# A second Strassen level for the last product of a down projection, with helper work moved to GpSimd

## The chip, the cores and the metric

The kernel runs on one core of one Trainium2 chip. The metric is the device time of one execution in microseconds, lower is better. I use two measures side by side: the ratio of timed runs (with a 95% interval), and the lengths of the program's stages on TensorE's timeline.

The engines are called PE (TensorE matmul), PEld (its weight loads), DVE (VectorE), ACT (ScalarE), POOL (GpSimd) and SP (the queue that issues the DMAs) in profile lines. SBUF is the on-chip memory that holds the operands; PSUM is the memory that TensorE writes its results to, in banks. In the lines of the down stage, `ps` stands for PSUM, `RE` for the partial results `U` and `V`, `RO` for sums on their way to an output, `RX` for residual and output tiles, `RAB` for operand sums and for the outputs of product 5.

## The reference, cut to what matters

```python
def reference(A_x, A_wqkv, A_wo, B_x, B_W_gate, B_W_up, B_W_down):
    ...
    x = A_x                                            # [1, 2048, 1024] bf16
    h = x + _A_ref(_layernorm(x), A_wqkv, A_wo)        # linear attention, 32 heads
    h2 = h + _B_ref(_layernorm(h), B_W_gate, B_W_up, B_W_down)
    return h2
# _B_ref: gate, up = x @ W_gate, x @ W_up  (1024 x 3584); (relu(gate) * up) @ W_down  (3584 x 1024)
```

Only the last product, with `W_down`, and the addition of `h` are touched by the change.

## The kernel before

The token axis is handled in two passes of 1024 tokens. Each pass has a gate/up stage of 14 pairs of feature tiles (PE 12.09 us per pair), then a down stage. Every large product uses Strassen's scheme: seven half-size block products in place of eight. In the down stage the seven products run one after the other. Four are "direct" (56 matmuls with 512 columns); three are split a second time by the same scheme into seven half products of 14 matmuls with 256 columns ("level 2"). The program numbers the products 0 to 6.

Operands of level 2 are sums of blocks. Activation sums are made by VectorE during the down stage. Weight sums are made once, in gate/up pass 0, and stored to DRAM.

```python
            direct(0, XB, a_hh(0, 0), False, True, e_s1)
            level2(1, q_d2, sg_ro, ev(0, B_U, 0, B_U, "dU"))
            direct(2, XB, a_hh(1, 0), False, False, e_11)
            level2(3, q_hh(0, hh16), sg_x0, ev(STB, B_V, 0, B_U, "dV"))
            direct(4, XB, a_d1(), True, True, e_22)
            level2(5, q_hh(1, hh), sg_x0, ev_21)
            direct(6, XB, a_hh(1, 0, hh16), False, False, e_12)      # the product that the change splits
```

`U` and `V` are f32 partial results in SBUF. After product 4, VectorE adds the result banks to `V` (`e_22`), and GpSimd adds four residual tiles of `h` to make four outputs. The residuals for the two other output blocks are added into `V` and `U` by VectorE:

```python
            def e_22(j):
                h, hb = hv(1, 1, j)
                tt(dsum[:, j, :], bank(XB[j]), V_[j], [B_bank[XB[j]], B_V[j]], [B_dsum[j]], "d22")
                put(1, 1, j, dsum[:, j, :], h, [B_dsum[j], hb], "pool")
            ...
            def add_h(dst, bufs_, blk, dh):
                for j in range(STB):
                    h, hb = hv(blk, dh, j)
                    tt(dst[j], dst[j], h, [hb], [bufs_[j]], "dh")      # VectorE, two SBUF inputs
            ...
            at(4, 0, lambda: ld_h(1, 1))          # "after unit (product, part): load residual tiles"
            at(4, 2, lambda: ld_h(1, 0))
            ...
            at(5, 0, lambda: add_h(V_, B_V, 1, 0))
            at(5, 6, lambda: ld_h(0, 1))
            at(6, 2, lambda: add_h(U_, B_U, 0, 1))
```

Inside a level-2 product four PSUM banks are reused: a later half product goes on accumulating in a bank that VectorE reads, so PE may not start it before that read is over.

```python
                def m5():
                    prod(5, c, sg(0), False)
                    evac(5, c)
                ...
                def m3():
                    prod(3, c, sg(3), False)
                    evac(3, c)
                units.extend(((pi, i), f_) for i, f_ in enumerate((m1, m7, m6, m2, m5, m4, m3)))
```

The whole DMA work goes through one in-order queue (SP). Down-stage weights come through a ring of 7 slots in pass 0 and 13 in pass 1.

## Time and profile before

| | before |
|---|---|
| time, median of 3 | 737.76 us (737.58 to 738.92) |
| PE busy | 726.8 us, 99% of 737.5 |
| DVE, ACT, POOL busy | 544.3 us (74%), 350.4 us (48%), 61.3 us (8%) |
| one direct product, PE | 12.09 us |
| one level-2 product, PE | 10.70 us |

The page's first part gives the busy times and, after the `x`, the instructions:

```profile
PE 726.8 (99%) x4227; PEld 356.0 (48%) x4227; DVE 544.3 (74%) x972; ACT 350.4 (48%) x610; POOL 61.3 (8%) x125
```

A busy PE is not by itself a PE at its limit, but the timeline says more. In PE's timeline of down pass 0 (start, length in us, engine, line, operation, tiles, count, and in brackets idle time before it with its releaser) the end of the stage looks like this:

```profile
465.34 1.69 PE L687 MATMUL ps<-RAB 128*128 128x256 f16 x14
466.87 3.22 PE L687 MATMUL ps<-RE,RAB 128*128 128x256 f16 x28
469.93 9.46 PE L687 MATMUL ps<-RW,RAB 128*128 128x256 f16 x50
479.23 2.75 PE L687 MATMUL ps<-RAB 128*128 128x512 bf16 x12
481.82 1.89 PE L687 MATMUL ps<-RE,RAB 128*128 128x512 bf16 x8
484.08 1.90 PE L687 MATMUL ps<-RH,RWG 128*128 128x512 bf16 x8 [0.37 <-DVE RX L1399]
```

A half product starts 1.53 us after the one before it (465.34 to 466.87), and the only idle time is 0.37 us at the border to gate/up pass 1, where the first bank waits for the last output add. (A named idle time counts from the modelled end of the matmul before. Counted from start to start, the border costs 0.54 us; the waits of the down stage below are likewise about 0.16 us longer from start to start than named.) So each microsecond of matmul taken away should come off the time, unless another engine then arrives too late.

VectorE's and GpSimd's timelines show what those engines do around products 4 to 6 of pass 0 (VectorE first):

```profile
449.48 4.34 DVE L1399 TENSOR_TENSOR RAB<-RAB 128x1792 f16<-128x1792 bf16 x4
459.66 2.48 DVE L1399 TENSOR_TENSOR RO<-ps,RE 128x512 f32<-128x512 f32 x4 [5.85 <-PE ps L687]
462.24 4.79 DVE L1399 TENSOR_TENSOR RE<-RE,RX 128x512 f32<-128x512 f32 x4
...
479.79 2.50 DVE L1399 TENSOR_TENSOR RE<-RE,RX 128x512 f32<-128x512 f32 x4 [3.92 <-DMA RX<-h_scr]
```

```profile
460.49 5.39 POOL L1399 TENSOR_TENSOR RX<-RO,RX 128x512 bf16<-128x512 f32 x4 [93.63 <-DVE RO L1399]
```

The two `RE<-RE,RX` lines are the same four VectorE adds with two SBUF inputs. Beside GpSimd's adds (460.49 to 465.88) they take 4.79 us, without them 2.50 us. This is the trace's form of what the Trainium skill says in "SBUF — State Buffer", section "Who interferes with whom": a VectorE instruction with two SBUF inputs and a GpSimd instruction that reads SBUF exclude each other.

### The profile page before, as it was taken

How to read it: one execution, taken by the hardware profiler on the slowest of the kernel's cores; microseconds unless marked ns; L12 is line 12 of the kernel's file. 1: busy time of each engine (PE TensorE's matmuls, PEld its weight loads, DVE VectorE, ACT ScalarE, POOL GpSimd, SP SyncE). 2: the span in 40 equal slices, each digit the busy share in tenths (PEclk: the TensorE clock that was granted, in tenths of full speed). 3: DMA queues.
4: the chain of work that ended last, by engine and by line, in shares of the span. 5: the costliest groups of instructions: out<-in, count | busy, mean ns of one | idle time of the engine just before them, and what ended most of it. 6: DMA issues, size and time to landing. Idle time of an engine off the chain costs nothing.

```text
span 737.5 us, 11324 instructions
## 1 busy us (share of the span) xinstructions
PE 726.8 (99%) x4227; PEld 356.0 (48%) x4227; DVE 544.3 (74%) x972; ACT 350.4 (48%) x610; POOL 61.3 (8%) x125
## 2 busy tenths in 40 slices
PE   7999999999999999999999999999999999999998
PEld 3444444344444444444444666744444444447764
DVE  6886877799776988888987765775757575676563
ACT  3877756864841457777754100035454454521000
POOL 1311100000360001110100000200000000000020
PEclk9999999999999999999999999999999999999999
DMA  9635135113999887797869999952424242337872
GB/s 309 204 72 101 28 96 167 39 26 64 192 234 256 269 249 226 234 282 229 261 203 286 315 251 324 328 173 73 110 63 114 58 116 57 100 109 246 239 223 85
DMA packets 185302, 129.32 MB, mean 175 GB/s; under 512 B 51488, under 2 KB 168224, under 8 KB 185248
## 3 DMA queue, kind: packets, MB, share of 16 engines
q1 hardware_dynamic: 184576, 127.95, 61.5%
q8 instruction: 33, 0.54, 0.3%
q10 hardware_dynamic: 672, 0.66, 0.3%
q14 instruction: 21, 0.17, 0.1%
HBM read 93.72 MB, written 23.33 MB: 159 GB/s over the span
## 4 chain that ended last, share of the span: by engine, by line
PE 90%; DVE 5%; ACT 2%; DMA 2%; issue 1%; DVEq 0%; SPq 0%; ACTq 0%
PE ps L687 90%; DVE RAB L773 1%; ACT RX L766 1%; DVE RE L1148 1%; DMA RE<-in_A_x_dram 1%; DMA RAB<-RXH 1%; DVE RX L770 1%; DVE RX L989 0%; ACT ps L692 0%; ACT RXH L725 0%; PE ps L830 0%; DVE rden L1146 0%; DVE st L701 0%; DVE RX L1399 0%; DVE RWG L908 0%
## 5 line engine op out<-in xcount | busy, mean ns | idle before, releaser
L692 ACT ACTIVATE ps<-ps 128x512 f32<-128x512 f32 x168 | 97.8, 582 | 205.5 <-PE ps L687 145.6
L687 PE MATMUL ps<-RC,RO 128*128 128x512 f16 x672 | 154.2, 379 | 0.0
L687 PE MATMUL ps<-RH,RWG 128*128 128x512 bf16 x448 | 105.8, 379 | 0.4 <-DVE RX L1399 0.4
L687 PEld LDWEIGHTS ps<-RC,RO 128*128 128x128 f16 x672 | 65.8, 98 | 79.3
L1322 DVE TENSOR_TENSOR RAB<-ps,RAB 128x512 bf16<-128x512 f32 x56 | 38.6, 689 | 77.3 <-PE ps L687 77.3
L687 PE MATMUL ps<-RC,RWG 128*128 128x512 f16 x320 | 76.8, 379 | 0.1
L1318 DVE TENSOR_TENSOR RE<-ps,RE 128x512 bf16<-128x512 f32 x112 | 74.3, 684 | 1.7 <-PE ps L687 0.7
L687 PEld LDWEIGHTS ps<-RH,RWG 128*128 128x128 bf16 x448 | 43.8, 98 | 53.5 <-DVE RX L1399 0.9
L687 PE MATMUL ps<-RW,RAB 128*128 128x512 bf16 (+2 forms) x378 | 67.6, 336 | 0.0
L692 ACT ACTIVATE RE<-RE 128x512 bf16<-128x512 bf16 x56 | 35.1, 627 | 61.1 <-DVE RE L1318 60.5
L687 PE MATMUL ps<-RH,RO 128*128 128x512 bf16 (+1 forms) x256 | 61.2, 379 | 0.0
L687 PE MATMUL ps<-RW,RE 128*128 128x512 bf16 x256 | 57.5, 379 | 0.8 <-DVE RXH L1172 0.7
L687 PE MATMUL ps<-RAB 128*128 128x512 bf16 (+1 forms) x252 | 54.8, 357 | 0.0
L692 ACT ACTIVATE RE<-ps 128x512 f32<-128x512 f32 x64 | 37.7, 597 | 35.7 <-PE ps L687 35.3
L687 PEld LDWEIGHTS ps<-RW,RAB 128*128 128x128 bf16 (+1 forms) x378 | 37.0, 98 | 28.8
L687 PEld LDWEIGHTS ps<-RC,RWG 128*128 128x128 bf16 (+1 forms) x320 | 30.0, 98 | 39.9 <-ACT ps L692 5.9
L692 ACT ACTIVATE RAB<-ps 128x512 bf16<-128x512 f32 x56 | 33.4, 596 | 15.7 <-PE ps L687 14.6
L1266 DVE TENSOR_TENSOR RO<-RWG 128x1024 f16<-128x1024 bf16 x54 | 36.9, 683 | 4.7 <-DMA RWG<-in_B_W_up_dram 4.7
L1399 POOL TENSOR_TENSOR RX<-RO,RX 128x512 bf16<-128x512 f32 x8 | 10.8, 1379 | 338.4 <-DVE RO L1399 338.4
L687 PEld LDWEIGHTS ps<-RH,RO 128*128 128x128 f16 (+1 forms) x256 | 24.4, 98 | 30.1 <-ACT RX L692 1.6
L687 PEld LDWEIGHTS ps<-RW,RE 128*128 128x128 bf16 x256 | 23.9, 98 | 28.9 <-DVE RXH L1172 1.2
L1266 DVE TENSOR_TENSOR RO<-RWG,RO 128x1024 f16<-128x1024 bf16 x54 | 37.0, 686 | 1.0
(138 smaller groups left out, 944.0 us busy)
## 6 DMA issues: line engine op xcount, KB each, us to landing
RWG<-in_B_W_gate_dram SPq DMA_DIRECT2D x28, 512.0 KB, 4.8
RWG<-in_B_W_up_dram SPq DMA_DIRECT2D x28, 512.0 KB, 5.8
RW<-in_B_W_down_dram SPq DMA_DIRECT2D x14, 512.0 KB, 5.1
t_scr<-RW SPq DMA_DIRECT2D x14, 512.0 KB, 5.0
RE<-in_A_x_dram SPq DMA_DIRECT2D x23, 256.0 KB, 3.7
l_scr<-RX SPq DMA_DIRECT2D x7, 768.0 KB, 4.5
RW<-in_B_W_down_dram SPq DMA_DIRECT2D x14, 384.0 KB, 5.9
h_scr<-RXH SPq DMA_DIRECT2D x16, 256.0 KB, 3.3
```

The lines of the kernel that those rows point to most:

```text
L687: lambda e: e.matmul(out_ap, lhsT, rhs, start=start, stop=stop, skip_group_check=skip),
L692: PL.add("act", lambda e: e.activation(out=dst, in_=src, func=func), reads=reads, writes=writes, name=name)
L766: PL.add("act", lambda e: e.activation(out=Et[:, k, :], in_=src, func=ACTF.Exp), reads=[src_buf], writes=[B_E[k]], name=name + "_exp")
L770: PL.add("dve", lambda e: e.tensor_scalar(out=Et[:, k, :], in0=Et[:, k, :], scalar1=1.0, scalar2=1e-6, op0=ALU.min, op1=ALU.add), reads=[] ...
L773: PL.add("dve", lambda e: e.scalar_tensor_tensor(out=dst_ap, in0=src, scalar=C1, in1=Et[:, k, :], op0=ALU.add, op1=ALU.max), reads=[src_bu ...
L1148: PL.add("dve", lambda e: e.tensor_tensor(out=osb[:, k, :].rearrange("p (g h e) -> p g h e", h=HPG, e=Dh), in0=nv[:, :, :, 0:Dh], in1=rden ...
L1266: PL.add(eng, lambda e: e.tensor_tensor(out=tb(j, u), in0=f0(u), in1=f1(u), op=ALU.subtract), reads=[B_w[i + x] for x in r] + ([B_T[k + x] ...
L1318: PL.add("dve", lambda e: e.tensor_tensor(out=dst, in0=src, in1=ftmp[:, w, :], op=ALU.add), reads=[bsrc, B_s5[w]], writes=[bdst], name=name)
L1322: PL.add("dve", lambda e: e.tensor_tensor(out=dst, in0=a_, in1=b_, op=ALU.mult), reads=reads, writes=[wr], name=name)
L1399: PL.add(eng, lambda e: e.tensor_tensor(out=dst, in0=in0, in1=in1, op=op), reads=reads, writes=writes, name=name)
```

## The change

The intent: product 6 also gets a second level (56 x 512 columns become 7 x 14 x 256). Its weight sums are extra work in gate/up pass 0; they go to GpSimd because VectorE is busy there. The residual adds into `U` and `V` go to GpSimd, earlier than before, so that the outputs of products 5 and 6 can be written straight from PSUM.

```diff
-        WSRC = [("b", 0, 0), ("l", 1), ("b", 1, 0), ("l", 2), ("t", 0), ("l", 3), ("b", 1, 1)]
+        WSRC = [("b", 0, 0), ("l", 1), ("b", 1, 0), ("l", 2), ("t", 0), ("l", 3), ("l", 4)]
...                                      # in wd_sums (VectorE weight sums of one raw pair)
-            if q + NWR < NPAIR:
-                load_wraw(q + NWR)
...
+            def addw(j, x, y):
+                PL.add("pool", lambda e: e.tensor_tensor(out=lsw[:, z, j, :], in0=x[0], in1=y[0], op=ALU.subtract),
+                       reads=x[1] + y[1], writes=[B_lsw[z][j]], name="WM%d_%d" % (j, m))
+            def raw():
+                addw(0, wr(0, 1), wr(0, 0))
+                addw(2, wr(1, 1), wr(0, 1))
+                addw(1, wr(1, 1), t_(0))
+                addw(3, wr(1, 0), t_(1))
+                dma(sl_lw[z], l_v[:, no, :, m, :], lsw[:, z], "st_wm_%d" % m, reads=B_lsw[z], writes=[B_wscr[m]])
...
-                    tt(dst[j], dst[j], h, [hb], [bufs_[j]], "dh")
+                tt(dst[j], dst[j], h, [hb], [bufs_[j]], "dh", eng="pool")
...
-            direct(6, XB, a_hh(1, 0, hh16), False, False, e_12)
+            level2(6, XB, q_d4, sg_x1, ev_out(0, 1, 0, B_U, outst, B_outst, sl_out))
...
-            at(4, 0, lambda: ld_h(1, 1))
+            at(3, 4, lambda: ld_h(0, 1))
+            at(4, 0, lambda: ld_h(1, 1), *[lambda j=j: add_h(U_, B_U, 0, 1, j) for j in range(STB)])
             at(4, 2, lambda: ld_h(1, 0))
-            for i in range(4):
-                at(4, i, sg4[i])
-            at(5, 0, lambda: add_h(V_, B_V, 1, 0))
-            at(5, 6, lambda: ld_h(0, 1))
-            at(6, 2, lambda: add_h(U_, B_U, 0, 1))
+            for i, f_ in enumerate(sg4 + sg3):
+                at(4, i // 2, f_)
+            order = (2, 3, 0, 1)
+            at(5, 0, *[lambda j=j: add_h(V_, B_V, 1, 0, j) for j in order], *[lambda j=j: p_22(j) for j in range(STB)],
+               lambda: e_u5(0), lambda: e_u5(1))
+            at(5, 1, lambda: e_u5(2), lambda: e_u5(3))
+            at(5, 4, st_flush)
```

VectorE now has eight operand sums during product 4 (`sg4 + sg3`) where it had four. The raw rows of `W_down` are loaded two at a time, after GpSimd has read the pair before.

More of the change, by code (lines that the diff above doesn't have):

```diff
@@ L199, in bass_sequential_preLN__linear_attn_block__glu_gated_reglu__prompt_kernel @@
     t_v = t_scr.rearrange("(o p) (q c) -> p o q c", p=P, c=NW)
-    l_scr = nc.dram_tensor("l_scr", [len(L2O) * 4 * P, WDW], f16).ap()
+    l_scr = nc.dram_tensor("l_scr", [(len(L2O) + 1) * 4 * P, WDW], f16).ap()
     l_v = l_scr.rearrange("(o j p) (m c) -> p o j m c", p=P, j=4, c=HNW)
@@ L238, in bass_sequential_preLN__linear_attn_block__glu_gated_reglu__prompt_kernel @@
         hh = RAB[:, 0:NFT * TOK].rearrange("p (a b) -> p a b", a=NFT)
-        wdx = RAB[:, NFT * TOK + 4 * SBW:NFT * TOK + 4 * SBW + WDW]
+        wdx = RAB[:, NFT * TOK + 4 * SBW:NFT * TOK + 8 * SBW]
+        lsw = wdx.bitcast(f16).rearrange("p (s j c) -> p s j c", s=2, j=4)
         o0 = NFT * TOK
@@ L253, in bass_sequential_preLN__linear_attn_block__glu_gated_reglu__prompt_kernel @@
         wo = RW[:].rearrange("p (a b) -> p a b", a=NG)
-        wdring = [RW[:, i * WDW:(i + 1) * WDW] for i in range(NWS - 3)] + [wdx]
+        wdring = [RW[:, i * WDW:(i + 1) * WDW] for i in range(NWS - 3)] + [wdx[:, 0:WDW]]
         D2 = RC[:, 0:NPAIR * SBW].bitcast(f16).rearrange("p (q t) -> p q t", t=SBW)
@@ L372, in bass_sequential_preLN__linear_attn_block__glu_gated_reglu__prompt_kernel @@
         sl_ls = slots("dls_", 2)
+        sl_lw = slots("dlw_", 2)
         sl_out = slots("dout_", NOS)
@@ L433, in bass_sequential_preLN__linear_attn_block__glu_gated_reglu__prompt_kernel @@
         B_lscr = bufs("lscr_", NM)
+        B_lsw = [bufs("lsw%d_" % i, 4) for i in range(2)]
+        B_wscr = bufs("wscr_", NM)
         B_sgo = bufs("sgo_", 4)
@@ L472, in bass_sequential_preLN__linear_attn_block__glu_gated_reglu__prompt_kernel @@
             b_.over = B_wraw + flat(B_wsum)
-        B_wd[NWS - 3].over = flat(B_xnT) + flat(B_pqT)
+        for b_ in flat(B_lsw):
+            b_.over = flat(B_xnT) + flat(B_pqT)
+        B_wd[NWS - 3].over = flat(B_lsw)
         for b_ in B_wd[NWS - 2:NWS]:
@@ L614, in load_wd_next @@
             if src[0] == "l":
-                dst = dst.rearrange("p (m c) -> p m c", c=HNW)
+                dst = dst[:, 0:WDW].rearrange("p (m c) -> p m c", c=HNW)
                 o = src[1]
-                if src[2] == "q":
+                if src[2] == "q" and o == 4:
+                    k, h = src[3:]
+                    dma(sl_wd[i], wdring[i].rearrange("p (m c) -> p m c", c=HNW),
+                        wd_v[:, 1, k:NPAIR:2, NW + h * HNW:NW + (h + 1) * HNW], "ld_wr_%d" % L, writes=[B_wd[i]])
+                elif src[2] == "q":
                     k, h = src[3:]
@@ L621, in load_wd_next @@
                 else:
-                    dma(sl_wd[i], dst, l_v[:, L2O.index(o), src[3]], "ld_wl_%d" % L, reads=B_lscr,
+                    dma(sl_wd[i], dst, l_v[:, o - 1, src[3]], "ld_wl_%d" % L, reads=B_wscr if o == 4 else B_lscr,
                         writes=[B_wd[i]])
@@ L679, in half, with wr, t_ @@
                     add(3, wq_(1, 0), t(1))
-                    dma(sl_ls[z], l_v[:, :, :, m, :], lsum[:, z], "st_wl_%d" % m, reads=B_lsum[z],
+                    dma(sl_ls[z], l_v[:, 0:no, :, m, :], lsum[:, z], "st_wl_%d" % m, reads=B_lsum[z],
                         writes=[B_lscr[m]])
-            return [lambda: half(0), lambda: half(1)]
+            def wr(k, h):
+                return wraw[:, (2 * m + k) % NWR, 1, NW + h * HNW:NW + (h + 1) * HNW], [B_wraw[(2 * m + k) % NWR]]
+            def addw(j, x, y):
+                PL.add("pool", lambda e: e.tensor_tensor(out=lsw[:, z, j, :], in0=x[0], in1=y[0], op=ALU.subtract),
+                       reads=x[1] + y[1], writes=[B_lsw[z][j]], name="WM%d_%d" % (j, m))
+            def raw():
+                def t_(j):
+                    return lsw[:, z, j, :], [B_lsw[z][j]]
+                addw(0, wr(0, 1), wr(0, 0))
[3 more added lines that the diff above has]
+                dma(sl_lw[z], l_v[:, no, :, m, :], lsw[:, z], "st_wm_%d" % m, reads=B_lsw[z], writes=[B_wscr[m]])
+            return [lambda: half(0), lambda: half(1), raw]
         def mm(out_ap, lhsT, rhs, start, stop, reads, bbuf, name, skip=False):
@@ L1383, in bass_sequential_preLN__linear_attn_block__glu_gated_reglu__prompt_kernel @@
         X0v = hh16[:, 0:NFT:2, 0:SBW]
+        X1v = hh16[:, 0:NFT:2, SBW:2 * SBW]
         def down_pass(ps_, fill):
@@ L1431, in e_22, with p_22, e_u5, add_h @@
             def e_22(j):
+                tt(dsum[:, j, :], bank(XB[j]), V_[j], [B_bank[XB[j]], B_V[j]], [B_dsum[j]], "d22")
+            def p_22(j):
                 h, hb = hv(1, 1, j)
-                tt(dsum[:, j, :], bank(XB[j]), V_[j], [B_bank[XB[j]], B_V[j]], [B_dsum[j]], "d22")
                 put(1, 1, j, dsum[:, j, :], h, [B_dsum[j], hb], "pool")
-            def e_12(j):
-                put(0, 1, j, bank(XB[j]), U_[j], [B_bank[XB[j]], B_U[j]])
-            def add_h(dst, bufs_, blk, dh):
-                for j in range(STB):
-                    h, hb = hv(blk, dh, j)
-                    tt(dst[j], dst[j], h, [hb], [bufs_[j]], "dh")
+            def e_u5(j):
+                tt(U_[j], bank(XB[j]), U_[j], [B_bank[XB[j]]], [B_U[j]], "dU5")
+            def add_h(dst, bufs_, blk, dh, j):
+                h, hb = hv(blk, dh, j)
+                tt(dst[j], dst[j], h, [hb], [bufs_[j]], "dh", eng="pool")
             def quad(base, T, H):
@@ L1452, in l2_add, with l2_out @@
                    bd[2 * T:2 * T + 2], name)
-            def l2_out(T, H, b):
-                tt(out2[:, 2 * T:2 * T + 2, H * HNW:(H + 1) * HNW], qb(b), quad(STB, T, H),
-                   [B_bank[b]] + B_V[2 * T:2 * T + 2], B_out2[2 * T:2 * T + 2], "out21_%d%d" % (T, H))
+            def l2_out(ost, bo, base, bs, T, H, b):
+                tt(ost[:, 2 * T:2 * T + 2, H * HNW:(H + 1) * HNW], qb(b), quad(base, T, H),
+                   [B_bank[b]] + bs[2 * T:2 * T + 2], bo[2 * T:2 * T + 2], "out_%d%d" % (T, H))
             def a_hh(k, t, f=hh):
@@ L1499, in sg_x0, with sg_x1, q_d4 @@
                 return X0v[:, b0:b0 + NM, c0:c0 + SHB], [B_hh[2 * (b0 + m)][0] for m in range(NM)]
+            def sg_x1(j):
+                b0, c0 = NM * (j // 2), (j % 2) * SHB
+                return X1v[:, b0:b0 + NM, c0:c0 + SHB], [B_hh[2 * (b0 + m)][1] for m in range(NM)]
+            def q_d4(k, t):
+                i0 = 2 * k + 1
+                return hh16[:, i0:NFT:4, t * SHB:(t + 1) * SHB], [B_hh[i][0] for i in range(i0, NFT, 4)]
             units = []
@@ L1523, in go @@
                                 evac(j)
-                                if pi == 6:
-                                    st_flush()
                         else:
@@ L1531, in direct, with level2 @@
                     units.append(((pi, ci), go))
-            def level2(pi, Q, sg, evac):
-                a, f, b, c = YB
+            def level2(pi, bks, Q, sg, evac):
+                a, f, b, c = bks
                 def prod(mi, bk, x, start):
@@ L1539, in prod @@
                     wd_use[0] += 1
-                    w = wdring[ws].bitcast(f16)
+                    w = wdring[ws]
+                    if pi != 6 or mi in (5, 6, 7, 4):
+                        w = w.bitcast(f16)
                     for m in range(NM):
@@ L1594, in ev, with ev_out, out, st @@
                 return go
-            def ev_21(m, b):
-                if m == 2:
-                    l2_out(0, 0, b)
-                elif m == 7:
-                    l2_add(STB, B_V, STB, B_V, 1, 1, b, "dV2")
-                    l2_add(STB, B_V, STB, B_V, 1, 0, b, "dV2")
-                elif m == 5:
-                    l2_out(1, 1, b)
-                elif m == 4:
-                    l2_out(1, 0, b)
-                    for j in (2, 3):
-                        st_out(1, 0, j, sl_out2[j], out2[:, j, :], B_out2[j])
-                elif m == 3:
-                    l2_out(0, 1, b)
-                    for j in (0, 1):
-                        st_out(1, 0, j, sl_out2[j], out2[:, j, :], B_out2[j])
+            def ev_out(blk, dh, base, bs, ost, bo, sl):
+                def out(T, H, b):
+                    l2_out(ost, bo, base, bs, T, H, b)
+                def st(T):
+                    for j in (2 * T, 2 * T + 1):
+                        st_out(blk, dh, j, sl[j], ost[:, j, :], bo[j])
+                def go(m, b):
+                    if m == 2:
+                        out(0, 0, b)
+                    elif m == 7:
+                        l2_add(base, bs, base, bs, 1, 1, b, "dA")
+                        l2_add(base, bs, base, bs, 1, 0, b, "dA")
+                    elif m == 5:
+                        out(1, 1, b)
+                    elif m == 4:
+                        out(1, 0, b)
+                        st(1)
+                    elif m == 3:
+                        out(0, 1, b)
+                        st(0)
+                return go
             direct(0, XB, a_hh(0, 0), False, True, e_s1)
-            level2(1, q_d2, sg_ro, ev(0, B_U, 0, B_U, "dU"))
+            level2(1, YB, q_d2, sg_ro, ev(0, B_U, 0, B_U, "dU"))
             direct(2, XB, a_hh(1, 0), False, False, e_11)
-            level2(3, q_hh(0, hh16), sg_x0, ev(STB, B_V, 0, B_U, "dV"))
+            level2(3, YB, q_hh(0, hh16), sg_x0, ev(STB, B_V, 0, B_U, "dV"))
             direct(4, XB, a_d1(), True, True, e_22)
-            level2(5, q_hh(1, hh), sg_x0, ev_21)
-            direct(6, XB, a_hh(1, 0, hh16), False, False, e_12)
+            level2(5, YB, q_hh(1, hh), sg_x0, ev_out(1, 0, STB, B_V, out2, B_out2, sl_out2))
+            level2(6, XB, q_d4, sg_x1, ev_out(0, 1, 0, B_U, outst, B_outst, sl_out))
             post = {}
@@ L1638, in down_pass @@
             at(0, 3, sg6[3])
+            sg3 = l2_sums(q_d4, sg_x1, "sg3")
             at(2, 0, lambda: ld_h(0, 0))
-            for key in ((3, 1), (5, 1), (5, 6), (6, 0)):
+            for key in ((3, 1), (5, 6), (6, 0), (6, 6)):
                 at(*key, st_flush)
@@ L1878, in bass_sequential_preLN__linear_attn_block__glu_gated_reglu__prompt_kernel @@
                         if x % 2 == 1:
-                            w0_, w1_ = wl_sums(x // 2)
+                            w0_, w1_, wr_ = wl_sums(x // 2)
                             mid[1].append(w0_)
                             wl_q.append(w1_)
+                            mid[0].append(wr_)
+                            for z in (x + 1, x + 2):
+                                if z < NPAIR:
+                                    mid[0].append(lambda z=z: load_wraw(z))
                     if q not in wt_at:
```

## The prediction

The recorded texts count the products from one: their fifth product is product 4, their sixth is product 5.

> **What bounds the kernel.** TensorE. The page gives PE 726.8 of 737.5 us busy (99%) at a granted clock of 0.998, the chain of waits is 90% PE, and the list of waits holds only about 6.8 us of named PE waits, nearly all before 181 us. From there on PE idles once: 0.37 us at 483.7 us, between down pass 0 and gate/up pass 1, on VectorE's last output add. VectorE (74%), ScalarE (48%) and GpSimd (8%) have room. DMA is not free everywhere: in the stretches of down pass 0 (403 to 484 us) its busy share is 0.93 to 1.14 at about 255 to 325 GB/s; in gate/up pass 0 it is 0.86; at the end of pass 1 only 0.27.
>
> **What the change removes.** The last of the seven Strassen products, 56 matmuls of 512 columns per pass, becomes seven half-size products, 98 matmuls of 256 columns. The PE timeline shows both kinds: a direct product advances at 0.2159 us per matmul, 12.09 us in all; a second-level half product takes 1.528 us (starts 415.19, 416.72, 418.25), so seven take 10.70 us. Weight loads double to 98 but already hide in the existing second-level products (PE idle 0.0). Saving: 1.39 us per pass, 2.8 us in two, all on the critical path. I also expect the 0.37 us gap to go: bank 0 is now emptied four half products before the end. At the very end VectorE now has one add (0.69 us) after the last matmul where it had a queue of four ending 1.3 us after it: 0.2 to 0.5 us.
>
> **What it adds.** (1) GpSimd: 28 weight sums of 256 columns in gate/up pass 0, about 0.6 us each (estimate from the trace's 1.157 us for 512 columns), 17 us; and eight more 1.35 us residual adds per down pass. The Trainium skill ("SBUF — State Buffer", Who interferes with whom) says that a VectorE instruction with two SBUF inputs and a GpSimd instruction that reads SBUF shut each other out. The trace agrees: four such VectorE adds took 4.79 us beside GpSimd at 462 us and 2.50 us alone at 480 us. A gate/up pair has 1.2 to 2.4 us of VectorE idle, against at most 2.4 us of GpSimd sums every second pair: I expect 0 to 0.5 us of PE idle there. (2) DMA: 1.8 MB of stores in gate/up pass 0 (hidden), and weights of the last product 3.2 MB instead of 1.8 MB. (3) In down pass 0 the weight ring is seven ahead and the queue issues in order. The four stores of the GpSimd outputs now stand before the last two weight loads; VectorE has eight 1.09 us sums instead of four in the fifth product, blocked in part by four GpSimd adds, and GpSimd then runs eight adds in series (about 11 us). So the stores go 13 to 16 us after the fifth product's end, the next load lands 4 to 6 us later, and is due at 18.3 us: 0 to 3 us of PE wait, about 1 us expected. Pass 1 has thirteen slots: no wait.
>
> **Sum.** 2.8 + 0.4 + 0.3 − 1.0 − 0.3 = 2.2 us: 735.5 us. Range 734.0 to 737.0. Chances: faster by over 2% 0.01, within 2% 0.97, slower 0.02.
>
> **What would show it.** Last product about 10.7 us of PE in both passes; no gap at the pass boundary; VectorE sums of the fifth product stretched beside GpSimd; a PE wait on a weight load, if any, in the last two half products of pass 0 only; gate/up stretches equal within 0.5 us.
>
> **What would make it wrong.** VectorE, held by GpSimd, delaying gate/up (slower); the late loads waiting longer than 3 us; or neither costing anything (734.2).

## The result, and the profile after

The changed kernel took 736.48 us (median of 4 runs, 735.53 to 737.34), the kernel before 737.67 us (4 runs, 736.38 to 738.92). The ratio is 0.9984 with a 95% interval of 0.9962 to 1.0005: 1.2 us less, not clear of noise. Ratios in this document are the mean time of one kernel's fast runs over that of the other's fast runs of the same rounds, so they are not quite the ratio of the medians.

```profile
PE 720.8 (98%) x4253; PEld 363.2 (49%) x4311; DVE 561.6 (76%) x976; ACT 352.0 (48%) x614; POOL 103.7 (14%) x169
```

(PE has 84 matmuls more in the program, 4311; the trace lacks 58 of their records.) The list of PE's waits (line and tile, releaser; us in total, times, longest) now has entries from the middle of the program, where before there was one of 0.4 us:

```profile
PE ps L710 <- DVE RE L1341: 1.6, 2, 1.1
PE ps L710 <- DVE RAB L1423: 1.0, 1, 1.0
PE ps L710 <- DMA RW<-in_B_W_down_dram: 0.4, 1, 0.4
```

Lines have moved: L710 is the matmul helper (L687 before), L1423 the down stage's elementwise helper (L1399), L1341 the gate/up result adds (L1318), L677 and L655 the VectorE weight sums (L669, L645), L1289 the gate/up weight sums (L1266).

**The stages.** The table gives stage lengths from PE's timeline of each profile: from the first matmul of gate/up pass 0 to the first of down pass 0, and so on; "tail" is from the last matmul to the end. Where the trace lacks the first matmul of a group, its start is taken from the group before plus 0.216 us per matmul. A down stage with four level-2 products and no waits would take 3 x 12.09 + 4 x 10.70 = 79.07 us.

| us | gate/up 0 | down 0 | gate/up 1 | down 1 | tail | first gate/up matmul to the end |
|---|---|---|---|---|---|---|
| before | 169.21 | 80.98 | 169.22 | 80.45 | 3.78 | 503.64 |
| after | 170.89 | 80.80 | 169.22 | 79.35 | 3.60 | 503.86 |

So the two profiles, which differ by 2.6 us in span (737.5 and 734.9), do not differ after the first gate/up matmul, except for 0.2 us in the wrong direction. The 2.9 us lie in the start: the first gate/up matmul stands at 233.89 us before and at 231.01 us after, and 2.4 us of that are there already at the first matmul of the K projection (26.82 and 24.41 us), long before anything that the change touches. The runs below ask whether that is luck.

**Gate/up pass 0** is 1.68 us longer. In pair 2 PE waits for a VectorE result add:

```profile
266.34 1.67 PE L710 MATMUL ps<-RH,RO 128*128 128x512 bf16 x7 [0.50 <-DVE RE L1341]
```

VectorE just before that wait, in the kernel before and after (its timelines), and GpSimd (after):

```profile
261.93 1.14 DVE L669 TENSOR_TENSOR RX<-RW,RX 128x768 f16<-128x768 f16 x2
262.99 1.54 DVE L645 TENSOR_TENSOR RW<-RW 128x512 f16<-128x512 bf16 x4
265.24 0.69 DVE L1322 TENSOR_TENSOR RAB<-ps,RAB 128x512 bf16<-128x512 f32 x1 [0.71 <-PE ps L687]
```

```profile
260.35 1.49 DVE L677 TENSOR_TENSOR RX<-RW,RX 128x768 f16<-128x768 f16 x2
261.77 2.49 DVE L655 TENSOR_TENSOR RW<-RW 128x512 f16<-128x512 bf16 x4
264.18 0.68 DVE L1345 TENSOR_TENSOR RAB<-ps,RAB 128x512 bf16<-128x512 f32 x1
```

```profile
260.64 0.79 POOL L694 TENSOR_TENSOR RAB<-RW 128x256 f16<-128x256 bf16 x1 [2.09 <-DMA RW<-in_B_W_down_dram]
261.39 1.79 POOL L694 TENSOR_TENSOR RAB<-RW,RAB 128x256 f16<-128x256 bf16 x2
```

The same six VectorE instructions grew from 2.68 to 3.98 us while GpSimd's sums ran; before, VectorE then had 0.71 us to spare, after it none. They are not the whole of it: counted from the first gate/up matmul, VectorE came to them 1.3 us later than before (29.34 against 28.04 us), because GpSimd's first group of sums, at 242.23 to 245.99 us, had slowed it already, and its timeline shows no idle time after that in which it could catch up.

In pair 12 it happens again. PE's wait there (after), and the first two of the VectorE instructions above, before and after:

```profile
388.30 1.67 PE L710 MATMUL ps<-RH,RO 128*128 128x512 bf16 x7 [1.14 <-DVE RE L1341]
382.79 1.14 DVE L669 TENSOR_TENSOR RX<-RW,RX 128x768 f16<-128x768 f16 x2
381.68 1.61 DVE L677 TENSOR_TENSOR RX<-RW,RX 128x768 f16<-128x768 f16 x2
```

Pair 12 is also the one in which VectorE has least room. In the kernel before it is busy 11.88 of 12.09 us there (the columns of this view are explained under x_late), where most pairs leave it 1.24 to 2.34 us idle:

```profile
378.93:391.02 12.09, 12.09 (x58) 5.48 (x57) 11.88 (x26) 5.86 (x10) 0.00 (x0) 1.00 0.73 217
```

**Down pass 0** gained 1.39 us for the product and 0.54 us for the gap at the border, and gave nearly all of it back in products 5 and 6. VectorE, GpSimd and PE, from their timelines after:

```profile
448.28 12.22 DVE L1423 TENSOR_TENSOR RAB<-RAB 128x1792 f16<-128x1792 bf16 x8
460.41 2.48 DVE L1423 TENSOR_TENSOR RO<-ps,RE 128x512 f32<-128x512 f32 x4
462.81 1.28 DVE L1423 TENSOR_TENSOR RE<-ps,RE 128x512 f32<-128x512 f32 x2
466.02 2.61 DVE L1423 TENSOR_TENSOR RE<-ps,RE 128x512 f32<-128x512 f32 x4 [1.94 <-POOL RE L1423]
```

```profile
451.39 7.03 POOL L1423 TENSOR_TENSOR RE<-RE,RX 128x512 f32<-128x512 f32 x4 [69.11 <-DMA RX<-h_scr]
463.72 4.50 POOL L1423 TENSOR_TENSOR RE<-RE,RX 128x512 f32<-128x512 f32 x4 [5.30 <-DMA RX<-h_scr]
```

```profile
469.88 1.70 PE L710 MATMUL ps<-RW,RAB 128*128 128x256 f16 x14 [0.99 <-DVE RAB L1423]
472.00 4.76 PE L710 MATMUL ps<-RW,RAB 128*128 128x256 bf16 x42 [0.41 <-DMA RW<-in_B_W_down_dram]
```

Read from the bottom: `m3` of product 5 (469.88) waited for VectorE's read of its bank; VectorE was late because it waited 1.94 us for GpSimd's adds into `V`; GpSimd started these at 463.72, when a residual load landed. There are two candidates for "too late": VectorE's eight sums, which took 12.22 us where four took 4.34 before, and the load. The second wait, 0.41 us, is on a weight load.

### The profile page after: what moved, and what is told of

The parts are those of the page before. It is cut to its first block, busy times and chain, and to the rows that moved or that the text cites. A ratio compares the mean times of both kernels' runs of the same rounds, so it can differ in the third digit from the quotient of the medians.

```text
span 734.9 us, 11505 instructions
## 1 busy us (share of the span) xinstructions
PE 720.8 (98%) x4253; PEld 363.2 (49%) x4311; DVE 561.6 (76%) x976; ACT 352.0 (48%) x614; POOL 103.7 (14%) x169
## 4 chain that ended last, share of the span: by engine, by line
PE 82%; DVE 9%; DMA 3%; issue 2%; ACT 2%; SPq 1%; POOL 1%; POOLq 0%; DVEq 0%; ACTq 0%
PE ps L710 82%; DMA RW<-in_B_W_down_dram 1%; DVE RAB L796 1%; DVE RE L1171 1%; ACT RX L789 1%; DMA RX<-h_scr 1%; DVE st L724 1%; DMA RAB<-RXH 1%; DVE RX L793 1%; SPq L541 1%; DVE RX L1012 1%; DVE RO L1289 1%; POOL rstd L734 0%; DVE RW L906 0%; ACT ps L715 0%
## 5 line engine op out<-in xcount | busy, mean ns | idle before, releaser
L715 ACT ACTIVATE ps<-ps 128x512 f32<-128x512 f32 x172 | 100.1, 582 | 213.5 <-PE ps L710 162.0
L710 PE MATMUL ps<-RC,RO 128*128 128x512 f16 x672 | 154.3, 379 | 0.0
L710 PE MATMUL ps<-RH,RWG 128*128 128x512 bf16 x447 | 105.6, 379 | 0.1
L710 PEld LDWEIGHTS ps<-RC,RO 128*128 128x128 f16 x672 | 65.7, 98 | 79.5 <-ACT ps L715 0.5
L710 PE MATMUL ps<-RC,RWG 128*128 128x512 f16 x320 | 76.8, 379 | 0.3 <-ACT ps L715 0.3
L1341 DVE TENSOR_TENSOR RE<-ps,RE 128x512 bf16<-128x512 f32 x112 | 74.2, 684 | 1.6 <-PE ps L710 0.7
L710 PEld LDWEIGHTS ps<-RH,RWG 128*128 128x128 bf16 x448 | 43.9, 98 | 52.6
L710 PE MATMUL ps<-RW,RAB 128*128 128x256 f16 (+3 forms) x412 | 66.8, 318 | 1.5 <-DVE RAB L1423 1.0
L1423 POOL TENSOR_TENSOR RE<-RE,RX 128x512 f32<-128x512 f32 x16 | 23.1, 1473 | 307.5 <-DMA RX<-h_scr 307.5
L710 PE MATMUL ps<-RH,RO 128*128 128x512 bf16 (+1 forms) x228 | 55.3, 379 | 3.0 <-DVE RE L1341 1.6
L710 PE MATMUL ps<-RW,RE 128*128 128x512 bf16 x243 | 56.6, 380 | 1.5 <-DVE RXH L1195 0.7
L710 PE MATMUL ps<-RAB 128*128 128x512 bf16 (+2 forms) x268 | 57.6, 351 | 0.4
L710 PEld LDWEIGHTS ps<-RW,RAB 128*128 128x128 bf16 (+1 forms) x414 | 40.4, 98 | 25.8 <-DVE RAB L1423 1.3
L710 PEld LDWEIGHTS ps<-RC,RWG 128*128 128x128 bf16 (+1 forms) x320 | 30.0, 98 | 40.2 <-ACT ps L715 6.2
L1289 DVE TENSOR_TENSOR RO<-RWG 128x1024 f16<-128x1024 bf16 x54 | 39.7, 736 | 4.7 <-DMA RWG<-in_B_W_up_dram 4.7
L1423 DVE TENSOR_TENSOR RE<-ps,RE 128x512 f32<-128x512 f32 x40 | 27.0, 687 | 18.9 <-PE ps L710 15.6
L715 ACT ACTIVATE RAB<-ps 128x512 bf16<-128x512 f32 x56 | 33.4, 596 | 14.7 <-PE ps L710 13.6
L710 PEld LDWEIGHTS ps<-RH,RO 128*128 128x128 f16 (+1 forms) x256 | 24.2, 98 | 31.8 <-DVE RE L1341 2.2
L710 PEld LDWEIGHTS ps<-RAB 128*128 128x128 bf16 (+1 forms) x274 | 26.3, 98 | 25.2 <-ACT RAB L856 1.1
```

The source lines that it names most:

```text
L710: lambda e: e.matmul(out_ap, lhsT, rhs, start=start, stop=stop, skip_group_check=skip),
L715: PL.add("act", lambda e: e.activation(out=dst, in_=src, func=func), reads=reads, writes=writes, name=name)
L1289: PL.add(eng, lambda e: e.tensor_tensor(out=tb(j, u), in0=f0(u), in1=f1(u), op=ALU.subtract), reads=[B_w[i + x] for x in r] + ([B_T[k + x] ...
L1341: PL.add("dve", lambda e: e.tensor_tensor(out=dst, in0=src, in1=ftmp[:, w, :], op=ALU.add), reads=[bsrc, B_s5[w]], writes=[bdst], name=name)
L1423: PL.add(eng, lambda e: e.tensor_tensor(out=dst, in0=in0, in1=in1, op=op), reads=reads, writes=writes, name=name)
```

## The experiments

Theory A: VectorE and GpSimd shut each other out when both read two SBUF inputs, and this is what delays VectorE. Theory B, the rival: loads land too late, those of the raw weight rows in gate/up pass 0 (the change loads them later) and the residual load in the down stage. All edits are to the changed kernel. Each group of runs shared runs of the kernel before on the same chip (9 to 11 of them), five or six runs per kernel.

All stage lengths in one place (us):

| run | gate/up 0 | down 0 | down 1 | first gate/up matmul to the end | ratio to before (95%) |
|---|---|---|---|---|---|
| r_before | 169.21 | 81.22 | 80.43 | 503.89 | 1.0006 (0.9994 to 1.0018) |
| r_after | 170.45 | 80.56 | 79.18 | 503.00 | 0.9987 (0.9974 to 1.0000) |
| x_raw (wrong result) | 169.21 | 80.63 | 79.06 | 501.70 | 0.9963 (0.9951 to 0.9975) |
| x_late | 169.21 | 79.53 | 79.50 | 501.07 | 0.9961 (0.9949 to 0.9973) |
| x_dve_sums | 169.79 | 79.32 | 79.26 | 501.18 | 0.9967 (0.9955 to 0.9979) |
| x_swap_h | 170.90 | 79.91 | 79.05 | 502.68 | 0.9982 (0.9969 to 0.9995) |
| x_u_dve | 170.69 | 80.85 | 79.60 | 503.94 | 0.9995 (0.9979 to 1.0010) |
| v_a | 169.21 | 81.21 | 79.06 | 502.28 | 0.9973 (0.9957 to 0.9989) |
| v_b | 169.21 | 79.78 | 79.05 | 500.84 | 0.9951 (0.9938 to 0.9963) |
| v_c | 169.22 | 80.97 | 79.06 | 502.04 | 0.9959 (0.9947 to 0.9971) |
| v_alldve | 169.59 | 81.30 | 82.96 | 506.67 | 1.0032 (1.0012 to 1.0052) |
| v_vpool | 169.60 | 79.38 | 79.05 | 500.85 | 0.9958 (0.9944 to 0.9971) |

Gate/up pass 1 is 169.21 to 169.23 us in every one of them.

### r_after and r_before: is the early start luck?

Both kernels again, unaltered.

> The changed kernel itself again, unaltered, timed in more rounds. The two profiles at hand start 2.4 us apart in the first matmuls, before anything that the change touches. From the stages after that, the change should be worth nothing: gate/up pass 0 is 1.7 us longer, down pass 0 0.2 us shorter, down pass 1 1.1 us shorter. If those stages repeat and the start is luck, the ratio is 0.999 to 1.001; if the start is part of the change, it stays near 0.997 and the first gate/up pair starts near 231 us again, not 234.

> The kernel before, as a kernel of its own, for a second profile and for the noise of the ratio. Stages after the start repeat within 0.1 us: gate/up 169.2, down 81.0 and 80.45, 503.6 us from the first gate/up matmul to the end. The start (first gate/up matmul at 233.9 us in the one profile) is the part that varies: if it is luck, it comes out between 231 and 233 here; if it belongs to the kernel, near 234. Ratio 0.999 to 1.001.

In the second profile of the kernel before, the first gate/up matmul stands at 232.18 us, not 233.89, and the first matmul of the K projection at 24.45 us, as in the others. The late start of the first profile was luck. Its stages repeated to 0.02 us, except down pass 0, where the gap at the border was 0.62 us instead of 0.37. The changed kernel's stages repeated in kind (170.45, 80.56 and 79.18 us). By stages the changed kernel is between 0.9 us better and 0.2 us worse than the kernel before; by the clock, 736.47 against 737.86 us here, and the ratio of 0.9987 lies just outside the 0.999 to 1.001 that was expected if the start is luck. Both allow a gain of about 1 us. Its first gate/up matmul came at 232.02 us. Whether a few tenths of the start belong to the changed kernel, two profiles of the kernel before can't tell; it stays open.

### x_raw: no weight sums on GpSimd

```diff
-                addw(0, wr(0, 1), wr(0, 0))
-                addw(2, wr(1, 1), wr(0, 1))
-                addw(1, wr(1, 1), t_(0))
-                addw(3, wr(1, 0), t_(1))
-                dma(sl_lw[z], l_v[:, no, :, m, :], lsw[:, z], "st_wm_%d" % m, reads=B_lsw[z], writes=[B_wscr[m]])
+                for k in range(2):
+                    i = (2 * m + k) % NWR
+                    dma(sl_lw[k], l_v[:, no, 2 * k:2 * k + 2, m, :],
+                        wraw[:, i, 1, NW:2 * NW].bitcast(f16).rearrange("p (j c) -> p j c", j=2),
+                        "st_wm_%d_%d" % (m, k), reads=[B_wraw[i]], writes=[B_wscr2[m][k]])
```

> Wrong result on purpose: the 28 GpSimd weight sums are gone; the raw weight rows are stored in their place, same bytes to the same addresses, and the next raw rows are loaded only after that store. Theory A (VectorE and GpSimd shut each other out when both read two SBUF inputs): gate/up pass 0 falls back from about 170.9 to 169.2 us, both PE waits on VectorE there go, VectorE's 128x512 weight sums of pair 12 and pair 2 are 0.38 us each again; time 1.5 to 1.7 us less than the changed kernel. Theory B (the later loads of the raw rows hold VectorE up): the loads are as late or later here, so the two waits stay, 1 us or more.

The result is wrong, as intended. Gate/up pass 0 fell to 169.21 us, to the hundredth what it was before the change, and both waits went, although the raw rows still come late (the third of them lands 26.5 us after the first gate/up matmul, 26.8 us in the changed kernel and 17.9 us before). This refutes theory B for this stage. The median fell from 736.47 to 735.39 us, a little less than expected, and the ratio by 0.24%. The waits of product 5 stayed.

### x_late: the same sums, at another time

```diff
-                addw(0, wr(0, 1), wr(0, 0))
+                addw(0, wr(0, 1), (wr(0, 0)[0], wr(0, 0)[1] + [B_wsum[(2 * m + 1) % NWR][3]]))
```

The first sum of each group now also waits for VectorE's last sum of the same pair of rows.

> The same 28 GpSimd weight sums, but each group of four now waits for VectorE's last sum of the same pair of rows, so that it runs in the odd gate/up pair, after VectorE's eight sums' worth of work there, not early in the even pair before. Theory A with placement (a group hurts only where VectorE has no idle time left, pairs 2 and 12): the wait of pair 2 (0.5 us) goes, that of pair 12 (1.15 us) falls to 0.5 or less; gate/up pass 0 takes 169.2 to 169.8 us instead of 170.5 to 170.9. Rival, that GpSimd sums cost their time wherever they stand: it stays above 170.4. Raw rows are loaded still later, so a theory of late raw loads says longer, not shorter.

Gate/up pass 0: 169.21 us, with no wait at all, for the same 28 GpSimd instructions. Six of the seven groups of four now run in the odd pairs 1 to 11. The last stayed in pair 12, but ran at 385.11 to 388.23 us, mostly beside VectorE adds that read PSUM, and cost PE nothing. VectorE in pair 2 is back at its old durations and its spare time:

```profile
260.07 1.15 DVE L677 TENSOR_TENSOR RX<-RW,RX 128x768 f16<-128x768 f16 x2
261.13 1.55 DVE L655 TENSOR_TENSOR RW<-RW 128x512 f16<-128x512 bf16 x4
263.09 0.69 DVE L1345 TENSOR_TENSOR RAB<-ps,RAB 128x512 bf16<-128x512 f32 x1 [0.41 <-PE ps L710]
```

How much VectorE is held can be read from its busy time between the first matmul of gate/up pass 0 and the first of down pass 0, in the windows view of before, after, x_raw and x_late, in this order (the columns are the window, its length, then busy us and instruction counts of PE, PEld, DVE, ACT and POOL, the clock, DMA share and GB/s):

```profile
233.89:403.10 169.21, 169.21 (x785) 76.72 (x784) 140.99 (x274) 108.10 (x180) 13.05 (x32) 1.00 0.83 248
```

```profile
231.01:401.90 170.89, 168.62 (x772) 76.50 (x784) 149.12 (x274) 107.53 (x180) 34.37 (x60) 1.00 0.87 255
```

```profile
231.80:401.01 169.21, 168.48 (x771) 76.61 (x784) 141.09 (x274) 108.08 (x180) 13.06 (x32) 1.00 0.86 259
```

```profile
231.74:400.95 169.21, 169.21 (x785) 76.71 (x784) 142.41 (x274) 107.59 (x180) 32.01 (x60) 1.00 0.87 257
```

With the same 274 instructions, VectorE counts 8.1 us more busy time in the changed kernel than before (149.12 against 140.99): a blocked instruction counts as busy. With the sums held back it counts only 1.4 us more. So the cost is one of placement. The ratio fell to 0.9961, from 0.9987. Not all of that is the gate/up stage: down pass 0 was also 1.0 us shorter than in r_after, which this edit does not aim at (see x_swap_h).

### x_dve_sums: the sums on VectorE

```diff
-                PL.add("pool", lambda e: e.tensor_tensor(out=lsw[:, z, j, :], in0=x[0], in1=y[0], op=ALU.subtract),
+                PL.add("dve", lambda e: e.tensor_tensor(out=lsw[:, z, j, :], in0=x[0], in1=y[0], op=ALU.subtract),
```

> The 28 weight sums on VectorE instead of GpSimd, in the same place of its program; everything else as in the changed kernel. About 0.26 us each (estimate from 0.38 us for 512 columns), 7 us more VectorE work in gate/up pass 0 in exchange for about 1.8 us of blocking per group. If offloading them was right, VectorE falls behind: two or more waits of 1 us, pass above 171 us. If Theory A is right, VectorE loses no more by doing four sums (1.05 us) than by being blocked (1.8 us): pass 169.2 to 170.3, one wait at most, in pair 12.

Gate/up pass 0 took 169.79 us with one named wait, 0.22 us in pair 12. VectorE doing the 28 sums costs PE less (0.58 us) than GpSimd doing them at a bad time (1.2 to 1.7 us), and more than GpSimd doing them at a good one (0).

### x_swap_h: exchange two residual loads

```diff
-            at(4, 0, lambda: ld_h(1, 1), *[lambda j=j: add_h(U_, B_U, 0, 1, j) for j in range(STB)])
-            at(4, 2, lambda: ld_h(1, 0))
+            at(4, 0, lambda: ld_h(1, 0), *[lambda j=j: add_h(U_, B_U, 0, 1, j) for j in range(STB)])
+            at(4, 2, lambda: ld_h(1, 1))
```

The first load goes to slots that are free; the second needs slots that the four adds into `U` are still reading. GpSimd wants `h(1,0)` first.

> Only the order of two residual loads is exchanged, so that the residual which GpSimd adds first after the fifth product is loaded first. Theory B for the down passes (GpSimd's second four adds wait for their load): they start 1.3 us earlier in pass 0 (at the end of VectorE's third sum with V instead of at the load's landing), the wait of the sixth product's last half product falls from 1.15 us in pass 0 and 0.3 us in pass 1 to 0 to 0.2, time about 1 us less. Theory A alone (VectorE was late because of the port): at most 0.3 us less. The gate/up stretch keeps its 1.7 us in both.

GpSimd's adds into `V` and VectorE after them, in pass 0 (timelines):

```profile
463.65 4.50 POOL L1423 TENSOR_TENSOR RE<-RE,RX 128x512 f32<-128x512 f32 x4 [3.95 <-DVE RO L1423]
```

```profile
465.95 2.61 DVE L1423 TENSOR_TENSOR RE<-ps,RE 128x512 f32<-128x512 f32 x4 [0.59 <-POOL RE L1423]
```

GpSimd is now released by VectorE and no longer by the load, VectorE waits 0.59 us instead of 1.94, and `m3` of product 5 doesn't wait for VectorE in either pass. Down pass 1 is 79.05 us, the length without waits. Down pass 0 keeps 0.84 us over 79.07; two waits on weight loads, 0.34 and 0.18 us, are named. So in the down stage it was theory B: the load, not the blocked sums. The gain is 0.65 us in down pass 0 and 0.13 in down pass 1 against r_after, below the 1 us expected: in r_after `m3` was 0.89 us late where the first profile had 1.16, and in x_swap_h a wait on a weight load still makes it 0.51 us late. By the clock the ratio (0.9982) is not told apart from r_after's.

The traces of the other runs say the same of the load. In all six with the old order (after, r_after, x_raw, x_late, x_dve_sums, x_u_dve) GpSimd starts its adds into `V` 0.13 us after the third tile of that load lands (the adds begin with tile 2), and in pass 0 `m3` starts 6.2 us after GpSimd. Counted from product 5's start, in that order: GpSimd 4.17, 3.89, 4.57, 3.24, 3.25 and 4.81 us, `m3` 10.33, 10.06, 10.73, 9.42, 9.42 and 10.97 us, where 9.17 us would be without a wait. So the wait follows the landing, and the landing moves by 1.6 us between runs although the order of the queue is the same. x_late and x_dve_sums lost only 0.25 us here without the exchange; why their loads landed earlier was not tested.

### x_u_dve: the adds into U on VectorE

```diff
-            at(4, 0, lambda: ld_h(1, 1), *[lambda j=j: add_h(U_, B_U, 0, 1, j) for j in range(STB)])
+            at(4, 0, lambda: ld_h(1, 1))
...
+                if i == 3:               # in the middle of VectorE's eight sums
+                    at(4, 1, *[lambda j=j: add_h(U_, B_U, 0, 1, j, "dve") for j in range(STB)])
```

> Only the four residual adds into U, which run on GpSimd beside VectorE's eight operand sums of the fifth product, go back to VectorE. Theory A: the eight sums take 8.8 us instead of 12.2, the four adds 2.5 us on VectorE, so VectorE reaches the fifth product's evacuation about 0.9 us earlier in spite of having more to do. Theory B: the wait in the sixth product stays about 1 us, as GpSimd's next four adds still wait for their load at 463.7 us; Theory A alone says it goes.

VectorE's timeline:

```profile
448.31 4.33 DVE L1423 TENSOR_TENSOR RAB<-RAB 128x1792 f16<-128x1792 bf16 x4
452.57 2.49 DVE L1423 TENSOR_TENSOR RE<-RE,RX 128x512 f32<-128x512 f32 x4
454.98 4.34 DVE L1423 TENSOR_TENSOR RAB<-RAB 128x1792 f16<-128x1792 f16 x4
459.23 2.48 DVE L1423 TENSOR_TENSOR RO<-ps,RE 128x512 f32<-128x512 f32 x4
```

Eight sums and four adds together take 10.9 us (448.31 to 459.23) where the eight sums alone took 12.1 us beside GpSimd. Four adds moved away from VectorE cost it 3.5 us of blocking; doing them costs 2.5 us. Theory A is right about the mechanism, but this part of it was not on the critical path: GpSimd's adds into `V` still waited for their load (to 464.40 us), down pass 0 stayed at 80.85 us, and the ratio did not fall.

### v_a, v_c: moving the stores; v_b: the two repairs alone

v_b is x_late and x_swap_h together. v_a is v_b with a group of output stores sent one half product later, v_c is v_b with all eight stores of the outputs of products 4 and 5 sent after the last weight load of the pass:

```diff
-            at(5, 4, st_flush)
+            at(5, 5, st_flush)          # v_a;   v_c: the line is taken out, the stores go at (5, 6)
```

> A version meant to be faster: the exchanged residual loads, the GpSimd sums held to the odd pair, and the stores of the fifth product's second half sent one half product later, behind the weight load that PE waited for. Expected from the stages: gate/up pass 0 169.2 to 169.8, down pass 0 79.1 to 79.6, down pass 1 79.1; 500.9 to 501.5 us from the first gate/up matmul to the end against 503.6 of the kernel before and 503.0 to 503.9 of the changed one; ratio to before 0.995 to 0.997.

> The exchanged residual loads and the held GpSimd sums together, the stores left where the changed kernel has them. Gate/up pass 0 169.2 us, down pass 1 79.1, down pass 0 79.1 to 80.0 (waits for a DMA load up to 0.5 us may remain); 500.4 to 501.5 us from the first gate/up matmul to the end; ratio to before 0.9945 to 0.9965. If the two repairs overlap, it is not better than the held sums alone (501.06).

> As the one before, and all eight stores of the fifth and sixth products' outputs go behind the last weight load of the pass. One half product later they had stood in front of that last load, which cost 1.17 us; behind it no weight load of the pass waits for a store. Down pass 0 79.1 to 79.5 us. If instead the DMA engines themselves are the limit, a wait on a load of 0.5 us or more stays in down pass 0.

v_b has the lowest ratio here, though the intervals of v_c, v_vpool and x_late overlap with its own: 733.97 us (733.06 to 734.28) against 737.57 us of before in the same rounds, ratio 0.9951. By stages the exchanged loads added only 0.2 us to x_late (501.07 to 500.84), because in x_late's profile the load came early. Gate/up pass 0 has no wait, down pass 1 is at its floor, and down pass 0 is 0.71 us above it. Moving the stores did not help. In v_a, the last half product of product 6 waits for its weights, whose load now stands behind the stores:

```profile
480.93 1.69 PE L710 MATMUL ps<-RW,RAB 128*128 128x256 bf16 x14 [1.17 <-DMA RW<-in_B_W_down_dram]
```

That load was issued 13.6 us after product 5's start (472.55 us), 12.7 us in v_b, and took over 8 us to land while DMA was full. In v_c no weight load stood behind a store, yet PE waited 1.13 us for the first weight load of product 6, which was issued as early as in v_b (4.1 and 4.0 us after product 5's start); it also waited 0.44 us because VectorE could not overwrite the output tiles before their late stores. So, as the expectation for v_c put its alternative, the order of the queue is not all: what is left of down pass 0 depends on how fast the DMAs land in a stage where their share is about 1. I did not test that further. The three ratios (0.9973, 0.9951, 0.9959) are not all told apart by their intervals; the stages and the named waits are what the verdict rests on.

### v_alldve and v_vpool: was the offloading needed?

v_alldve is x_swap_h, x_u_dve and x_dve_sums together, with the adds into `V` on VectorE too: the arithmetic of the change with GpSimd as idle as before. v_vpool differs from it in one word:

```diff
-            at(5, 0, *[lambda j=j: add_h(V_, B_V, 1, 0, j, "dve") for j in order], ...      # v_alldve
+            at(5, 0, *[lambda j=j: add_h(V_, B_V, 1, 0, j) for j in order], ...             # v_vpool: GpSimd
```

> The arithmetic of the change alone: the seventh product by a second level, with every weight sum and the residual adds into U and V on VectorE, loads in the exchanged order; GpSimd keeps only the four adds that it had before. Was the offloading needed? If VectorE has the room, gate/up pass 0 169.2 to 169.9 us, down passes 79.1 to 79.8 and 79.1 us, and the ratio is that of the repaired GpSimd version, 0.995 to 0.997. If VectorE is too full, gate/up or the sixth product show waits on it of over 1 us.

> The version with everything on VectorE lost 2.1 us of PE wait in the sixth product of each pass, and in pass 1 the PE clock fell to half after that wait. Here only the four adds into V go back to GpSimd; the weight sums and the adds into U stay on VectorE. If what hurt was the four V adds on VectorE standing beside GpSimd's four output adds (4.4 us for four instead of 2.5), both waits go: down pass 1 79.1 us, down pass 0 79.1 to 79.9, gate/up pass 0 169.6 to 169.8, ratio 0.995 to 0.9965, no clock below 1. If what hurt was the U adds or the general load of VectorE, the waits stay at over 1 us.

v_alldve was slower than the kernel before (739.40 us, ratio 1.0032, interval above 1), against the expectation. Its VectorE and GpSimd around product 5:

```profile
460.29 4.41 DVE L1423 TENSOR_TENSOR RE<-RE,RX 128x512 f32<-128x512 f32 x4
```

```profile
461.17 5.67 POOL L1423 TENSOR_TENSOR RX<-RO,RX 128x512 bf16<-128x512 f32 x4 [97.16 <-DMA RX<-h_scr]
```

The adds into `V` now ran beside GpSimd's four output adds, both with two SBUF inputs, and took 4.41 us instead of 2.49. `m3` of product 5 waited 2.07 us for VectorE in both passes. In pass 1 more was lost, and the windows view shows where (clock is the third number from the end of a line):

```profile
717.00:718.00 1.00, 1.00 (x11) 0.74 (x8) 0.97 (x3) 0.00 (x0) 0.34 (x1) 1.00 0.40 138
718.00:720.20 2.20, 0.13 (x3) 0.03 (x2) 2.17 (x5) 0.00 (x0) 0.00 (x0) 1.00 0.17 60
720.20:721.70 1.50, 1.50 (x10) 1.20 (x11) 0.65 (x1) 0.00 (x0) 0.00 (x0) 0.69 0.00 0
721.70:723.20 1.50, 1.50 (x9) 1.07 (x8) 0.34 (x1) 0.00 (x0) 0.00 (x0) 0.50 0.52 175
723.20:724.80 1.60, 1.60 (x12) 1.24 (x10) 0.35 (x1) 0.00 (x0) 0.00 (x0) 0.70 0.22 75
```

After the 2.07 us wait the granted clock fell to 0.50, and only 31 matmuls passed in 4.6 us, where some 42 would have. Down pass 1 took 82.96 us: 2.07 of wait, and about 1.8 that the list of waits does not name. In pass 0 a wait of the same length did not lower the clock (1.00 in every window after it). The mean granted clock of the six timed runs was 0.995 (once), 0.998 (four times) and 1.00 (once), so the fall was not in one execution alone.

v_vpool moved the four adds into `V` to GpSimd and nothing else: both waits went, the clock stayed at 1.00, down pass 1 took 79.05 us and the ratio is 0.9958. Of the three things that the change put on GpSimd, this is the one that paid: these four adds run while VectorE reads PSUM (one SBUF input), so they block nobody, and they keep GpSimd's output adds from running beside VectorE's. (Leaving them on VectorE and moving GpSimd's output adds out of their way was not tried.) The adds into `U` and the weight sums did not have to be there; with them on VectorE, v_vpool needs 500.85 us after the first gate/up matmul, v_b 500.84.

## Why the prediction was right or wrong

The time was inside the range: 736.48 us, with 735.5 predicted and 734.0 to 737.0 as range. The sum came out through terms of which several were off, and that it stayed inside the range is in part luck: the first profile has 3.7 us of waits where 1.3 us were predicted, and by stages the gain was between -0.2 and 0.9 us, where 2.2 us were predicted.

- **The saving: right.** With no waits, down pass 1 fell from 80.45 to 79.05 us (x_swap_h, v_b, v_vpool): 1.40 us where 1.39 was predicted. The doubled weight loads cost nothing.
- **The gap at the border: right.** It was 0.37 us (0.62 in the second profile of before; 0.54 and 0.78 from start to start) and is gone.
- **The tail: right, at the low end.** 0.2 to 0.5 us were predicted; the tail fell from 3.78 and 3.79 us to 3.60 and 3.59, by 0.2.
- **VectorE against GpSimd in gate/up pass 0: the term that was mis-sized most.** The prediction: "I expect 0 to 0.5 us of PE idle there." Measured: 1.68 and 1.24 us. The mechanism was right (x_raw takes the loss away, x_late takes it away with the same sums). The step that failed is the setting of 1.2 to 2.4 us of VectorE idle time in a pair against 2.4 us of sums "every second pair". Most pairs do have that idle time, but pair 12 has 0.21 us and pair 1 has 0.59. GpSimd is not tied to a pair either: its groups ran at the border of pairs 0 and 1 and in pairs 2, 5, 7, 9, 11 and 12, the first, second and last of them as soon as their raw rows had landed. And what VectorE loses it carries along until it has idle time: in pair 2 the losses of the first two groups came together.
- **The late weight loads in down pass 0: in part.** "0 to 3 us of PE wait, about 1 us expected", in the last two half products. In the first profile there was one wait of 0.41 us (0.57 from start to start), on the first half product's weights; in r_after there were two, 0.16 and 0.22 us, the later one on the half product before the last. Smaller, and not always where predicted.
- **"Pass 1 has thirteen slots: no wait": right of the weight loads, wrong of the pass.** PE waited for no weight load there, but `m3` of product 5 waited 0.30 us for VectorE, and 1.16 us (0.99 named) in pass 0. The prediction traced GpSimd's eight adds forward only to the stores. It left out that the adds into `V` also gate VectorE, and VectorE gates the PSUM bank of `m3`. What released those adds was a residual load behind others in the queue (x_swap_h removes the wait in both passes), not, as my theory A would have had it, the blocked sums before them (x_u_dve shortens those and changes nothing).
- **The sum.** Predicted gain 2.2 us. By stages, the gross gain of about 3.5 us (two products 2.8, gap 0.5, tail 0.2) was given back by 3.7 us of waits in the first profile (1.68, 1.16, 0.57 and 0.30). In r_after, against the same first profile of before, 0.6 us of gain were left. By the clock the gain is 1.2 and 1.4 us of median, ratio 0.9984 and 0.9987. That the clock says a little more than the stages I leave open.

The predicted signs mostly appeared: last product 10.70 us in both passes, no gap, stretched VectorE sums (12.22 us where eight alone take 8.7). "Gate/up stretches equal within 0.5 us" did not.

## What to carry to other kernels

In these runs, elementwise work moved from VectorE to GpSimd was free where VectorE at that moment ran instructions with at most one SBUF input: four adds beside PSUM reads cost nothing that the traces show, four adds beside two-input sums cost VectorE 3.5 us, more than the 2.5 us of doing them itself. Decide when the helper's work runs, by a dependency if need be, and put it where the other engine has time to spare, looking at its fullest stretch and not at the usual one: a dependency alone took 1.2 to 1.7 us of PE wait away here. When work moves earlier, move its loads in the queue too, and follow each moved result to every buffer that it frees.

## What the Trainium skill lacked or had wrong

- "SBUF — State Buffer", section "Who interferes with whom": right in kind; it gives no measured cost of a mix like this one. Here eight VectorE sums of 128x1792 took 12.22 us beside four GpSimd adds of 128x512 f32, against 8.67 us (4.33 and 4.34) without them. GpSimd was slowed as well: 7.03 us for its four against 4.50 us beside VectorE instructions with one SBUF input.
- "GPSIMD Engine Reference", section "Engine selection", says about 2x slower than VectorE for two-input operations. Here 1.8x for 128x512 f32 adds without interference (4.50 against 2.49 us for four). It does not say there that such an offload can cost VectorE more time than it saves, as x_u_dve shows (12.1 us of VectorE time against 10.9).
- "TensorE: Matmul & The Clock Gate", Part 1, has the clock fall after at least one idle window of about 3.4 us. In v_alldve it fell to 0.50 after a named wait of 2.07 us, and after a wait of the same length in the other pass it did not fall. One case; what sets them apart was not tested.
